# Feed-forward two slots earlier, with chunk 0's and 2's layer norm and w2's splits moved and w2's low halves on VectorE

## The chip, the cores and the metric

The kernel runs on one core of one Trainium2 chip. The metric is device time in microseconds (us) of one execution. Three runs of the kernel before were timed; their median counts. Beside them stands one profiled execution, from which all durations below come.

## The reference, cut to what matters

Inputs are 8 batches of 8 heads: 512 local queries, keys and values of width 64 per head, and 32 global ones. The result of an attention layer is mixed by a Fourier transform, normalised, and sent through a feed-forward pair of matrices.

```python
s_g = scale * q_g @ k_all^T;  out_g = sm(s_g) @ v_all          # 32 global rows see all 544 keys
s_ll = where(|i - j| <= 32, scale * q_l @ k_l^T, -1e9)          # local rows see a band
out_l = sm(concat(scale * q_l @ k_g^T, s_ll)) @ concat(v_g, v_l)
x = concat(out_g, out_l)                                        # [8, 544, 512]
u = x + real(fft(fft(x, axis=1), axis=2))
un = (u - mean(u)) / sqrt(var(u) + 1e-6)
out = u + max(un @ w_ch1, 0) @ w_ch2                            # 512 -> 2048 -> 512
```

Shapes here are those that the kernel works on (544 rows per batch).

## The kernel before, in words

**Arithmetic.** Nearly every operand of a matmul is a pair of float16 tiles, a high half (the value rounded) and a low half (what is left). A product takes three matmuls: high by high, high by low, low by high. So each operand needs a step that makes the high half (mostly ScalarE, ACT) and one that makes the low half (mostly GpSimd, POOL, for attention and weights; VectorE, DVE, for the transform and the feed-forward).

**The work.** Attention goes by 32 head pairs, each of four blocks of 128 queries; a block takes one *attention slot*. A batch has 16 slots, and six slots of pause stand after slot 15 (`A`). After the last slot of a batch (`E[b]`, attention slot 15 for batch 0, 37 for batch 1, 53 for batch 2) follows its transform: `d_load` to `d_add`, which adds the transform to x and so gives `u`. The rows of all batches are 17 *chunks* of 256 rows: chunks 2b and 2b+1 come from batch b, chunk 16 collects the rest. Each chunk has a layer norm (`l_stats`, `l_un`, `l_lo`, `l_turn`, and `l_root`, which refines the inverse root that is needed only at the end of the chunk, in `f_end`) and 16 *feed-forward slots* in 8 steps of two: `f_first` (24 matmuls, line 811), `f_hi`, `f_lo`, `f_second` (12 matmuls of 512 columns, line 830). `l_un` writes one tile of one buffer, `un`, so its second call (j = 1) waits until `l_lo` of the first has read it.

**The order.** It is written out by hand. Every step gets a time; `Plan.run` sorts by it and issues in that order, and each engine takes its own instructions strictly in that order. Times are plan slots. `add(slot, rank, ...)` puts a step at `warp(slot + rank)`, `at(time, ...)` at the time itself. `warp` leaves attention slots below `F0` as they are, stretches the next 23 over 32 plan slots, and gives two plan slots to each after those:

```python
late = F0 + 16 + PAUSE + LAG
def warp(t):
    if t < F0:
        return t
    return F0 + 32 * (t - F0) / (16 + PAUSE + LAG) if t < late else F0 + 32 + 2 * (t - late)
```

Chunk c's feed-forward begins at plan slot `F = F0 + 16 * c`; `f_first` of its step fp is at `F + 2 * fp + .30`, `f_second` at `F + 2 * fp + 3.30`. So a smaller `F0` moves all feed-forward earlier against attention: by about 2.8 plan slots of feed-forward in the stretch and four after it.

**Weights.** w1 and w2 come in as float64 bits and are turned into float32 by `w_load`, `w_abs`, `w_bits` during attention slots -11 to 30. `w_split` then scales 16 tiles of each (128x512): `w_hi` (line 252, ACT) writes the high half; for w1 POOL scales the tile and subtracts; for w2 (k = 1) ACT scales it in place (line 261) and POOL subtracts (line 262). w2's tile f is needed by `f_second` of chunk 0 in step f // 2.

**DMA.** All transfers are issued by SyncE (SP), in plan order too. `turn`, `g_turn` and `l_turn` are transposing DMAs; a DMA that waits for its source holds back those behind it on SP.

Of the kernel before, what the change touches and what calls it, by code (L numbers as in the profile page):

```python
# [13 lines left out]
AF = mybir.ActivationFunctionType  # L14
ALU = mybir.AluOpType
# [12 lines left out]
NVB = 2  # L28
NKB = 2
W0 = -8  # L30
F0 = 37
PAUSE = 6
LAG = 1
RS0 = 1.829591166069289e-20
# [41 lines left out]
class Plan:  # L76
# [3 lines left out]
    def add(self, slot, rank, fn, *a):  # L80
        self.at(self.warp(slot + rank), fn, *a)

    def at(self, time, fn, *a):
        self.q.append((time, len(self.q), fn, a))
# [6 lines left out]
class Kern:  # L91
# [163 lines left out]
    def w_split(self, k, i):  # L255
        nc = self.nc
        f, s, w = self.w_hi(k, i)
        if k == 0:
            nc.gpsimd.tensor_mul(f, f, s.to_broadcast([P, 512]))
        else:  # L260
            nc.scalar.activation(f, f, AF.Copy, scale=s)  # L261
        nc.gpsimd.tensor_sub(w[:, 1], f, w[:, 0])  # L262

    def b_load(self, b):
# [581 lines left out]
    def run(self):  # L846
        self.h = {}
# [7 lines that stand above are left out]
        plan = Plan(warp)  # L855
        add, at = plan.add, plan.at
# [3 lines left out]
        for n in range(32):  # L860
            k, t = divmod(n, 16)
            i = t if k else 4 * (t % 4) + t // 4
            s = W0 + (n if k == 0 else 16 + 3 * t // 2)
# [3 lines left out]
            if n % 4 == 3 and k == 0:  # L867
                c = n // 4
# [6 lines left out]
        add(s + 1, .62, self.w_fold)  # L875
        add(s + 2, .62, self.w_scale, 1, 0)
        for f in range(16):
            add(s + 3 + f, .75, self.w_split, 1, f)
        add(8, .09, self.load_consts)

        for b in range(B):
# [49 lines left out]
        for b in range(B):  # L931
# [32 lines left out]
            add(t + 2, .07, self.d_rest, b)  # L964
        at(F0 + 32 * 7 + 4.5, self.l_load)
        for c in range(17):
            F = F0 + 16 * c
            if c == 0:
                L, x, y, z = F - 4, (.50, .60), (.02, .06), (.30, .50)
            else:  # L970
                L, x, y, z = F - 6, (1.425, 2.425), (.335, .365), (.605, .605)
            at(L + .42, self.l_stats, c)
            for j in range(2):
                at(L + x[j], self.l_un, c, j)
                at(L + x[j] + y[1], self.l_lo, c, j)
                at(L + x[j] + z[j], self.l_turn, c, j)
            at(L + 3.43, self.l_root, c)
            for fp in range(8):
                t = F + 2 * fp
                at(t + .30, self.f_first, c, fp)  # L980
                at(t + .97, self.f_hi, c, fp)
                at(t + 1.20, self.f_lo, c, fp)
                at(t + 3.30, self.f_second, c, fp)
            for j in range(2):
                at(F + 17.82, self.f_end, c, j)
            at(F + 18.04, self.f_out, c)
# [52 lines left out]
```

## Time and profile before

| what | value |
|---|---|
| median of 3 runs | 1156.88 us |
| lowest and highest | 1155.44 and 1157.02 us |
| the profiled execution's own time | 1152.42 us |
| its span, first to last instruction | 1150.5 us |
| granted TensorE clock, mean | 0.941 |
| PE / DVE / ACT / POOL busy | 84% / 62% / 55% / 50% |
| first matmul of the feed-forward | 220.37 us |
| steps of `w_split` for w2 | 207 to 297 us |

The profile's page gives busy shares of the whole span; its rows of tenths give them by 40 slices of 28.8 us; the windows view gives busy microseconds of each engine in chosen stretches; the timeline lists instructions with their start and duration, and in brackets the idle time of the engine just before and what ended it; the chain of waits follows back from the last instruction what released what. L811 is line 811 of the kernel printed above. The profiled execution lies 4.5 us below the median of the runs.

### The profile page before, as it was taken

What the parts mean: (1) busy time and instruction counts of PE and PEld (TensorE: products, weight loads), DVE (VectorE), ACT (ScalarE), POOL (GpSimd) and SP (SyncE); (2) the same over time, 40 slices, a digit from 0 to 9 for tenths busy, and PEclk for the clock granted to TensorE, in tenths of its full rate; (3) what the DMA queues carried; (4) which work ended last, traced back from release to release, by engine and by line L of the source; (5) the groups of instructions that cost most, each with busy time, mean ns of one, the idle gap of its engine ahead of it and who ended that gap; (6) DMA issues with size and microseconds to landing.
All of it is one profiled execution on the core that took longest, in us unless ns stands there. A gap on an engine that the chain in (4) does not pass through costs nothing.

```text
span 1150.5 us, 25346 instructions
## 1 busy us (share of the span) xinstructions
PE 962.0 (84%) x9831; PEld 682.0 (59%) x9831; DVE 708.7 (62%) x1868; ACT 633.6 (55%) x1366; POOL 575.1 (50%) x728
## 2 busy tenths in 40 slices
PE   0244226588799899999999999999999999999996
PEld 0133215465576677676766676767677666666664
DVE  6997798547866865686568656866584444413211
ACT  5768558888676656665666566656564213212210
POOL 3789375778656554665465546654573312201100
PEclk9996557699899999999999999999999999999999
DMA  7578966567387465747465746573646212011100
GB/s 267 151 152 225 276 157 141 112 135 170 75 179 151 108 167 91 141 115 165 93 138 118 170 88 143 112 179 72 135 79 130 60 58 65 24 46 38 19 19 19
DMA packets 249569, 137.63 MB, mean 120 GB/s; under 512 B 200576, under 2 KB 223200, under 8 KB 249448
## 3 DMA queue, kind: packets, MB, share of 16 engines
q1 hardware_dynamic: 249448, 136.01, 51.2%
q8 instruction: 77, 1.26, 0.5%
q14 instruction: 44, 0.36, 0.1%
HBM read 65.10 MB, written 18.35 MB: 73 GB/s over the span
## 4 chain that ended last, share of the span: by engine, by line
PE 55%; DVE 24%; ACT 8%; DMA 6%; POOL 4%; issue 2%; SPq 0%; DVEq 0%; POOLq 0%; ACTq 0%
PE ps L811 22%; PE acc L830 22%; PE S L398 2%; DMA xt<-xs 2%; ACT pe L417 2%; DVE pe L408 2%; DMA qk<-in_qk 2%; PE bk L707 2%; DVE h L820 1%; PE S L468 1%; DVE ps L195 1%; DVE ps L196 1%; DVE z L328 1%; DVE wm L197 1%; DVE ps L194 1%
## 5 line engine op out<-in xcount | busy, mean ns | idle before, releaser
L811 PE MATMUL ps<-uh,wh 128*128 128x256 f16 x3264 | 383.4, 275 | 0.0
L830 PE MATMUL acc<-wh,h 128*128 128x512 f16 x1632 | 377.3, 381 | 4.1 <-DVE u L835 2.9
L811 PEld LDWEIGHTS <-wh 128*128 128x128 f16 x3264 | 319.2, 99 | 59.4 <-issue 0.7
L830 PEld LDWEIGHTS <-h 128*128 128x128 f16 x1632 | 153.5, 99 | 174.1 <-issue 9.2
L820 DVE SCALAR_TENSOR_TENSOR h<-ps,h 128x512 f16<-128x512 f32 x136 | 93.3, 686 | 188.6 <-ACT h L816 188.0
L425 POOL TENSOR_TENSOR ph<-pe,ph 128x448 f16<-128x448 f32 x128 | 137.2, 1072 | 143.0 <-ACT ph L421 88.5
L816 ACT ACTIVATE h<-ps 128x512 f16<-128x512 f32 x136 | 80.2, 589 | 223.4 <-PE ps L811 223.3
L417 ACT ACTIVATE pe<-pe,nm 128x224 f32<-128x224 f32 x256 | 102.0, 469 | 72.1 <-DVE nm L408 71.8
L408 DVE CUSTOM_DVE_ANT_0 pe<-S,msk,z 128x224 f32<-128x224 f32 x256 | 99.6, 445 | 7.5 <-PE S L398 3.6
L446 PE MATMUL bk<-vN,pl 128*128 128x65 f16 x768 | 72.9, 203 | 31.9 <-DMA pl<-ph 10.0
L398 PE MATMUL S<-kT,qT 64*128 64x192 f16 x768 | 55.7, 269 | 44.1 <-ACT pg L482 37.5
L398 PEld LDWEIGHTS <-qT 64*128 64x128 f16 x1536 | 53.7, 101 | 49.7 <-issue 38.9
L446 PEld LDWEIGHTS <-pl 128*128 128x128 f16 x768 | 62.2, 104 | 23.9 <-DMA pl<-ph 18.4
L421 ACT ACTIVATE ph<-pe 128x448 f16<-128x448 f32 x128 | 72.0, 562 | 0.0
L448 PEld LDWEIGHTS <-pl 96*128 96x128 f16 x768 | 60.1, 104 | 17.3 <-issue 10.5
L764 POOL TENSOR_SCALAR ve<-ve 128x2 f32<-128x2 f32 x17 | 5.8, 339 | 113.3 <-DVE ve L763 113.1
L376 POOL TENSOR_TENSOR kT<-qk,kT 128x512 f16<-128x512 f32 x32 | 40.7, 1272 | 36.4 <-ACT kT L371 33.0
L723 DVE SCALAR_TENSOR_TENSOR asm<-bk,dsc,asm 128x258 f32<-128x258 f32 (+1 forms) x21 | 10.1, 482 | 75.1 <-PE bk L707 60.5
L448 PE MATMUL bk<-vB,pl 96*128 96x65 f16 x576 | 55.2, 204 | 0.0
L774 ACT ACTIVATE un<-u,ve 128x512 f32<-128x512 f32 x34 | 27.6, 811 | 47.7 <-DVE unh L779 37.7
L361 ACT ACTIVATE qk<-qk,z 128x512 f32<-128x512 f32 x64 | 45.2, 708 | 10.7 <-DVE z L326 10.7
L262 POOL TENSOR_TENSOR wh<-wm,wh 128x512 f16<-128x512 f32 x32 | 38.0, 1188 | 19.7 <-ACT wm L261 18.3
(188 smaller groups left out, 1654.8 us busy)
## 6 DMA issues: line engine op xcount, KB each, us to landing
qk<-in_qk SPq DMA_DIRECT2D x32, 512.0 KB
vf<-in_v SPq DMA_DIRECT2D x32, 320.0 KB
raw<-in_moe_w_ch SPq DMA_DIRECT2D x18, 512.0 KB
xs<-x SPq DMA_DIRECT2D x32, 256.0 KB
out<-u SPq DMA_DIRECT2D x16, 512.0 KB
rw<-in_moe_w_ch SPq DMA_DIRECT2D x12, 512.0 KB
x<-xs SPq DMA_DIRECT2D x24, 256.0 KB
u<-xs SPq DMA_DIRECT2D x24, 256.0 KB
```

The lines of the kernel that those rows point to most:

```text
L361: self.nc.scalar.activation(s[nm], s[nm], AF.Copy, scale=s["z"][:, 3:4] if nm == "q" else s["z"][:, 4:5])
L398: nc.tensor.matmul(ps, qT[r, a, j], k, start=m == 0, stop=m == 2)
L408: nc.vector.tensor_tensor_reduce(self.per[(4 * p + j) % 4][:, h, 0:224], S[:, h, 224 * n:224 * n + 224], self.msk[:, j], z[:, 8:9], 3e38, ...
L417: nc.scalar.activation(pe[:, h, 0:224], pe[:, h, 0:224], AF.Exp, bias=nm[:, n, h:h + 1], scale=-1.0)
L421: self.nc.scalar.activation(ph[:, 0, :, 0:224], self.per[i % 4][:, :, 0:224], AF.Copy)
L425: self.nc.gpsimd.tensor_sub(ph[:, 1, :, 0:224], self.per[i % 4][:, :, 0:224], ph[:, 0, :, 0:224])
L446: nc.tensor.matmul(pv[:, j % 2, h], pl[:, 4 * a + 2 * h], vN[:, j, c, h, :], start=m == 0, stop=False)
L448: nc.tensor.matmul(pv[:, j % 2, h], pl[0:96, 4 * a + 2 * h + 1], vb, start=False, stop=m == 2)
L811: nc.tensor.matmul(ps[:, q], wt[:, w, c0:c0 + P], uh[:, :, 4 * a + kt, :], start=n == 0, stop=n == 11)
L816: self.nc.scalar.activation(h[:, 0], self.fps, AF.Relu)
L820: self.nc.vector.scalar_tensor_tensor(h[:, 1], self.fps, 0.0, h[:, 0], op0=ALU.max, op1=ALU.subtract)
L830: nc.tensor.matmul(self.acc_f[j], h[:, a, q, j * P:(j + 1) * P], self.w[1, f][:, w, :], start=f == 0 and a == 0 and w == 0, stop=f == 15 a ...
```

## The change

`F0` goes from 37 to 35. The low half of w2's tiles is made by one VectorE instruction, f * s - high, in place of ACT's scaling and POOL's subtraction. w2's splits are put at plan slots 33.75 + f directly, not through `warp`. Chunk 0's layer norm starts 2.82 plan slots ahead of its feed-forward (before: 4), with its two halves closer together; chunk 2's starts 4 ahead with its halves 0.1 apart (before: 6 ahead, one slot apart).

```diff
-F0 = 37
+F0 = 35
@@ w_split
         if k == 0:
             nc.gpsimd.tensor_mul(f, f, s.to_broadcast([P, 512]))
         else:
-            nc.scalar.activation(f, f, AF.Copy, scale=s)
+            nc.vector.scalar_tensor_tensor(w[:, 1], f, s, w[:, 0], op0=ALU.mult, op1=ALU.subtract)
+            return
         nc.gpsimd.tensor_sub(w[:, 1], f, w[:, 0])
@@ run
         for f in range(16):
-            add(s + 3 + f, .75, self.w_split, 1, f)
+            at(s + 3 + f + .75, self.w_split, 1, f)
@@ run
             F = F0 + 16 * c
             if c == 0:
+                L, x, y, z = F - 2.82, (.44, .50), (.02, .06), (.20, .30)
+            elif c == 2:
                 L, x, y, z = F - 4, (.50, .60), (.02, .06), (.30, .50)
             else:
                 L, x, y, z = F - 6, (1.425, 2.425), (.335, .365), (.605, .605)
```

In the last hunk `l_stats` is at L + .42, `l_un` of half j at L + x[j], `l_lo` at L + x[j] + .06 (y[1]), `l_turn` at L + x[j] + z[j], `l_root` at L + 3.43.

## Prediction

> **What bounds the kernel now.** I read the page's busy tenths first, then the windows view, then the timeline of each engine around the first feed-forward matmul, then the chain of waits up to 310 us.
>
> ```profile
> span 1150.5 us, 25346 instructions
> ...
> PE   0244226588799899999999999999999999999996
> ...
> PEclk9996557699899999999999999999999999999999
> ```
>
> The first row of tenths shows a kernel of two parts: up to about slice 10 PE is mostly idle, from there on it is full to the end. [...]
>
> ```profile
> 200.00:220.00 20.00, 6.96 (x91) 5.43 (x92) 13.12 (x42) 14.94 (x29) 13.16 (x16) 0.57 0.68 134
> 220.00:400.00 180.00, 158.93 (x1795) 113.67 (x1790) 122.69 (x338) 136.30 (x300) 125.52 (x147) 0.95 0.63 135
> 400.00:900.00 500.00, 486.76 (x5260) 345.55 (x5258) 327.00 (x879) 300.08 (x661) 278.23 (x351) 1.00 0.58 124
> 900.00:1100.00 200.00, 200.00 (x1485) 136.46 (x1485) 69.38 (x136) 43.68 (x74) 32.60 (x89) 1.00 0.15 41
> ```
>
> Columns are the stretch and its length, then busy us of PE, weight loads, DVE, ACT, POOL, then clock, DMA share, GB/s. PE idles 13.0 us in 200 to 220, 21.1 us in 220 to 400, 13.2 us in the 500 us after that, and nothing from 900 to 1100. The change leaves PE's work as it is, so the end moves by what PE's idle time changes, plus what matmuls cost at the low clock. All that can be won lies between 195 and 400 us. There the pace is set by ACT (76% busy in 220 to 400) and by engines that wait for each other.
>
> **Part 1: feed-forward two slots earlier, with chunk 0's layer norm.** These are PE's instructions around the first step:
>
> ```profile
> 219.13 0.67 PE L398 MATMUL S<-kT,qT 64*128 64x192 f16 x6 [3.25 <-ACT pg L482]
> ...
> 220.37 4.25 PE L811 MATMUL ps<-uh,wh 128*128 128x256 f16 x24
> ...
> 229.02 2.79 PE L811 MATMUL ps<-uh,wh 128*128 128x256 f16 x24
> ...
> 239.81 2.76 PE L830 MATMUL acc<-wh,h 128*128 128x512 f16 x12
> ```
>
> Scores 15 (plan slot 36.63) start at 219.13 after waiting 3.25 us for ACT; only then comes the first `f_first`, at 220.37. With F0 = 35 it is at plan slot 35.30, ahead of values 24 and scores 15, in the time when PE idles. Between scores 15 and scores 16 the new order then has two `f_first` and one `f_second` where the old one has a single `f_first`.
>
> But the layer norm that feeds it moves as well, from plan slot 33.42 to 32.60, right behind `d_add` of chunk 0 and ahead of slot 32's remaining work.
>
> ```profile
> 195.11 0.34 ACT L382 ACTIVATE kg<-gT,z 128x64 f16<-128x64 f16 x1
> ...
> 203.09 0.81 ACT L774 ACTIVATE un<-u,ve 128x512 f32<-128x512 f32 x1 [2.76 <-POOL ve L767]
> ...
> 205.32 0.82 ACT L774 ACTIVATE un<-u,ve 128x512 f32<-128x512 f32 x1 [0.76 <-DVE unh L779]
> ```
>
> ```profile
> 196.96 0.74 POOL L732 TENSOR_TENSOR u<-u,asm 128x255 f32<-128x255 f32 x1
> ...
> 202.84 0.21 POOL L767 TENSOR_SCALAR ve<-ve 128x2 f32<-128x2 f32 x1
> ```
>
> ```profile
> 198.60 0.69 DVE L760 BATCH_NORM_STATS2 bst<-u 128x6 f32<-128x512 f32 x1
> ...
> 207.22 0.68 DVE L779 TENSOR_TENSOR unh<-un,unh 128x512 f16<-128x512 f32 x1
> ```
>
> Before, ACT waits 2.76 + 0.76 = 3.5 us in the layer norm. In the new order its `l_un` stands right behind line 382, which ends at 195.45. POOL finishes chunk 0's u at 197.70; from DVE's first statistics (198.60) to POOL's last step (203.05) took 4.45 us, of which one half's 0.69 + 0.18 can go before 197.70, so the bias is there between 199.9 (nothing blocked) and 201.3. I take 200.0: ACT waits 4.5 us. Its second `l_un` waits for `l_lo`, which on DVE now stands behind w_scale, norm 10 and the four masked rows of slot 32; I estimate 2.3 us from their order. Together 6.8 us, 3.3 more than before. Queued behind it on ACT are prep_hi and sums of slot 32, `d_as`, exps 13, p_hi 25 and g_hi 6; DVE's `d_df` of the next block, PE's `d_second`, and scores 14 wait for those. POOL's three small steps move ahead of prep_lo, p_lo 25 and g_lo 6. On SP the two `l_turn` move ahead of turn 24, whose values are a slot and a half away on PE, so I put that at nothing, and at up to 1 us if that cover is gone. `l_root` goes to plan slot 35.61 and is needed only in `f_end`, over 16 slots later: nothing.
>
> ACT saves the three in-place scalings that stand ahead of scores 15 and gets one `f_hi`. The prices:
>
> ```profile
> L261 ACT ACTIVATE wm<-wm,wsc x16: 721/722/724, 207.4 to 295.4; 128x512 f32<-128x512 f32 x16
> ...
> L636 DVE SCALAR_TENSOR_TENSOR eh<-s,dsc,eh x8: 732/744/1525, 173.2 to 957.8; 128x512 f16<-128x512 f32 x8
> ...
> 362.84 0.58 ACT L816 ACTIVATE h<-ps 128x512 f16<-128x512 f32 x1
> ```
>
> So scores 15 move by 3.3 - 3 x 0.72 + 0.58 (an `f_hi`) = +1.7, to 220.8, and end at 222.1. Then PE does 2 x 2.79 + 2.76 = 8.3 us of feed-forward and about 3.3 us of values, global values and scores (the 8.65 us from 220.37 to 229.02 hold 4.25 of `f_first`, 2.1 us of waiting and some 2.3 of these; slot 26 and 27 with scores 16 make a little more in the new order): scores 16 end at 233.7, 4.7 us later than the 229.02 of before, but 8.3 us of feed-forward are ahead. **Term 1: -3.6 us**, from 0 (the layer norm costs another 3.6) to -6 (ACT's wait no longer than before and the POOL wait gone).
>
> **Part 2: w2's splits.** Sixteen ACT instructions of 0.722 us and sixteen POOL subtractions go; sixteen DVE instructions come. Line 636 has the same operation, size and types as the new one: 0.744 us. What of it lies on the path is to be read from the chain of waits:
>
> ```profile
> 273.60 1.16 POOL wh L262
> ...
> 294.67 0.73 ACT wh L252
> 295.43 0.72 ACT wm L261
> ```
>
> Three splits are in part 1; thirteen remain, 13 x 0.722 = 9.4 us off ACT and 13 x 1.16 = 15.1 us off POOL. Of that 1.16 + 0.73 + 0.72 = 2.6 us stand in the chain in the stretch where PE is worst fed (the last two because a split stands at plan slot 53; now all are done by 48.75, ahead of batch 1's transform). Between 220 and 245 more ACT pieces of splits stand in it, but other waits are next there. **Term 2: -3 us**, from 0 to -9.4 (all of ACT's time on the path).
>
> DVE gets 13 x 0.744 = 9.7 us in a stretch in which it idles 57 us of 180 (122.69 busy), so the work itself is covered; without that cover it would cost the 9.7. Each new instruction waits for ACT's high half, and masked rows, f_lo and g_max are queued behind it; but it stands 0.75 of a slot in, when DVE mostly waits for ACT anyway. The row of line 636 goes up to 1.525 us. [...] **Term 3: +0.3 us**, from 0 to +10 (13 x 0.78, the most by that row, all on the path).
>
> **Part 3: chunk 2.** With F0 = 35 `d_add` of batch 1 falls at 62.23 instead of 61.45, chunk 2's statistics stay at 63.42, its first matmul goes from 69.30 to 67.30: 5.07 slots from `d_add`, not 7.86.
>
> ```profile
> 331.34 0.84 POOL L731 TENSOR_TENSOR u<-u,asm 128x257 f32<-128x257 f32 x1 [1.90 <-DVE asm L724]
> ```
>
> From `d_add` (331.34) to the first `f_hi` of chunk 2, less a `f_first` of 2.8, are 28.7 us, 3.65 us per slot; 5.07 slots are 18.5 us. The chain needs 1.19 slots to the statistics (4.3 us), chunk 0's 9.3 us from 198.60 to the end of the second low half (207.90), and the transposing DMA, which I put at 3 to 4 us: 16.6 to 17.6. It just fits. ACT waits inside it as in chunk 0 (3.5 us), where ACT has a quarter of its time free. **Term 4: +1 us**, from 0 to +6. Even chunks from 4 on keep their layer norm, but `d_add` comes 1.28 slots ahead of the statistics, not 5.28; 4.7 us cover POOL's two adds of 0.84: nothing, at most 2 either way.
>
> **Part 4: the clock.** The first `f_first` took 4.25 us at the low clock, later ones 2.79. One such step stays. In the new order PE idles some 3 us between it and scores 15, so the second may be slow as well: **term 5: +0.7 us**, from 0 to +1.5. [...]
>
> **The sum:** -3.6 - 3 + 0.3 + 1 + 0.7 = -4.6 us. The profiled execution would go from a span of 1150.5 to 1145.9; its own time is 1152.42, 4.5 us below the median of the runs, and I carry the difference over: 1156.88 - 4.6 = 1152.3. About 0.2%, 2.3 us, can be told from no change.
>
> **The rivals.**
> (a) The layer norm gives all of term 1 back. For it: ACT is the pace maker at 200 to 245, and 6.8 us of waiting is my own estimate from the order. Against it: three scalings leave ACT at the same place. Then -3 + 2 = -1: 1156, no change to be told. Chance 0.14.
> (b) Slower: chunk 2's first matmul comes before its transposed rows. For it: the margin is 1 to 2 us. Against it: no slot of 3.65 us has to be lost for the chain to fit. It decides when the chain of part 3 passes 18.5 us, against 16.6 to 17.6 needed; then PE, which takes its queue in order, stands still for the excess. If the four DVE instructions in it take twice their 0.7 us, as line 636's slowest did, and ACT and SP reach it a slot late each (2 x 3.65), the chain is 17.6 + 2.8 + 7.3 = 27.7 us: 9.2 us of PE idle, so -4.6 - 1 + 9.2 = +3.6: 1160.5. Chance 0.12.
> (c) The new DVE instructions are blocked by POOL each time and hold the masked rows: 13 x 0.78 = 10.1 us, half of it on ACT's path, +5: 1157.3. Chance 0.05.
> (d) The splits are what feeds PE badly: all 9.4 us of ACT's time come off the path, -4.6 - 6.4 = -11: 1145.9. For it: ACT's share of the stretch; against: only 2.6 us of splits in the chain of waits after 245. Chance 0.14.
> (e) The forecast as worked out, within about 3 us: 0.55.
>
> **How the numbers follow.** Faster by over 0.2% holds (d) and most of the forecast, 0.66; within 0.2% (a), part of (c) and the forecast's upper edge, 0.19; slower (b) and part of (c), 0.15. The range takes in (a), (c) and (d) with an upper and lower edge of some 1.5 to 3 us beside them, and stops just short of (b): 1144.5 to 1160.
>
> **What would show it.** Right: the first L811 at about 211 to 213, slow; scores 15 at 220 to 222 with ACT idle some 4 us and 2 us ahead of its two L774; the new instructions at 0.75 to 1.5 us with no long wait of PE behind them; no PE wait at the first `f_first` of chunk 2; PE idle in 200 to 400 down by 4 to 6 us and unchanged after that. Wrong: scores 15 beyond 224, or a wait for the transposed rows at chunk 2, or PE idle that reappears after 400, where even chunks now follow their transform closely.

## The result, and the profile after

The change made the kernel slower: 1166.08 us median (1164.46 to 1169.2, 4 runs) against 1156.95 of the kernel before in the same comparison, a ratio of 1.0088, 95% interval 1.0065 to 1.0111. Forecast were 1152.3 and a range up to 1160.0.

The profiled execution of the changed kernel took 1169.2 us, 3.1 above its median, and that of before 4.5 below, so the two profiles differ by 16.8 us where the medians differ by 9.1. Differences between the two traces are read here for places and kinds; sizes come from the runs. The line numbers shown from 262 on are higher by one in the changed kernel.

The page (PEclk is the granted clock by slice, in tenths) and the windows view of the changed kernel, in the columns used for before:

```profile
span 1167.4 us, 25360 instructions
...
PE   0234326598689999989998999899989999999996
...
PEclk9999998699899999999999999999999999999998
```

```profile
200.00:220.00 20.00, 9.66 (x129) 8.02 (x128) 16.31 (x45) 10.39 (x21) 9.31 (x12) 0.67 0.53 86
220.00:400.00 180.00, 156.04 (x1762) 111.47 (x1762) 121.04 (x344) 124.34 (x279) 102.02 (x123) 0.93 0.62 138
400.00:900.00 500.00, 480.82 (x5089) 338.70 (x5087) 311.28 (x872) 302.17 (x667) 277.89 (x353) 0.98 0.56 121
900.00:1100.00 200.00, 199.00 (x1580) 136.38 (x1578) 74.41 (x161) 46.12 (x85) 38.64 (x86) 1.00 0.20 51
```

PE idles 10.3 us in 200 to 220 (13.0 before), 24.0 in 220 to 400 (21.1), and 19.2 in 400 to 900 (13.2). In the third row the granted clock is 0.98, not 1.00. The forecast looked for all of the effect ahead of 400 us; that part came out about even (34.3 us of idle time against 34.1), and the loss sits in the stretch that was taken to be full.

**Ahead of 310 us** the forecast steps happened, with two stalls that the forecast did not have. The first feed-forward step starts 8.8 us earlier, but scores 15 come 7.5 us later (219.13 before):

```profile
211.56 3.04 PE L812 MATMUL ps<-uh,wh 128*128 128x256 f16 x24
...
226.62 0.67 PE L399 MATMUL S<-kT,qT 64*128 64x192 f16 x6 [2.98 <-ACT pg L483]
```

ACT's waits in chunk 0's layer norm, from its timeline, are 4.5 and 1.3 us, close to the 4.5 and 2.3 worked out:

```profile
201.04 0.81 ACT L775 ACTIVATE un<-u,ve 128x512 f32<-128x512 f32 x1 [4.50 <-POOL ve L768]
...
203.80 0.81 ACT L775 ACTIVATE un<-u,ve 128x512 f32<-128x512 f32 x1 [1.29 <-DVE unh L780]
```

The extra stall stands in `scales` of group 4, eight tiny VectorE steps. First DVE's timeline of before, then that of the changed kernel, then POOL's of the changed kernel:

```profile
206.47 0.16 DVE L328 SCALAR_TENSOR_TENSOR z<-z 128x2 f32<-128x2 f32 x1
206.55 0.22 DVE L329 TENSOR_SCALAR z<-z,ge 128x2 f32<-128x2 f32 x1
206.81 0.17 DVE L330 TENSOR_SCALAR z<-z 128x4 f32<-128x4 f32 x1
```

```profile
209.73 0.98 DVE L329 SCALAR_TENSOR_TENSOR z<-z 128x2 f32<-128x2 f32 x1
210.64 2.72 DVE L330 TENSOR_SCALAR z<-z,ge 128x2 f32<-128x2 f32 x1
213.39 1.15 DVE L331 TENSOR_SCALAR z<-z 128x4 f32<-128x4 f32 x1
```

```profile
210.66 1.27 POOL L489 TENSOR_TENSOR pgr<-pg,pgr 64x576 f16<-64x576 f32 x1
211.89 0.73 POOL L732 TENSOR_TENSOR u<-u,asm 128x257 f32<-128x257 f32 x1
212.58 0.72 POOL L733 TENSOR_TENSOR u<-u,asm 128x255 f32<-128x255 f32 x1
213.27 1.24 POOL L341 TENSOR_TENSOR vf<-vf,z 128x640 f32<-128x640 f32 x1
```

Four of the eight steps, the three shown and the one behind them, last until a GpSimd instruction ends (at 210.69, 213.30, 214.51 and 215.50); the other four take 0.16 to 0.22 us. ACT's delay had held back POOL's work (p_lo 25, g_lo 6, `d_add`), which then came in one burst on top of `scales`: from 209.13 to 215.66 they take 6.5 us, where before they took 1.4 (205.88 to 207.31) and POOL stood idle beside them.

The second stall is PE's longest wait behind 200 us, in front of the scores at 304.42:

```profile
304.42 0.67 PE L399 MATMUL S<-kT,qT 64*128 64x192 f16 x6 [10.07 <-ACT pg L483]
```

The longest wait of before there was 6.04 us, at 290.64. In the changed kernel VectorE waits 4.74 us ahead of it for the transfer that `d_load` of batch 1 starts; before it waited 0.62.

**From 400 us on** the view of PE's waits says what is new. Its columns: who waited for whom, us in total, times, longest. First before, then the change, for 400 to 880 us:

```profile
PE bk L446 <- DVE xg L513: 5.4, 4, 1.4
PE bk L677 <- DVE x L459: 5.1, 3, 2.0
PE S L398 <- ACT pg L482: 1.9, 2, 1.6
```

```profile
PE S L399 <- ACT pg L483: 17.6, 5, 3.5
PE bk L447 <- DVE xg L514: 1.6, 4, 0.4
```

Several waits of 1 to 2 us became one of 3.52 us in each batch. One of the five, rows of three timelines of the changed kernel:

```profile
515.97 0.21 POOL L765 TENSOR_SCALAR ve<-ve 128x2 f32<-128x2 f32 x1 [10.24 <-DVE ve L764]
...
516.73 2.35 POOL L594 TENSOR_TENSOR s<-x 128x1020 f32<-128x1020 f32 x1
```

```profile
519.11 2.04 DVE L598 TENSOR_TENSOR x<-x 128x1020 f32<-128x1020 f32 x1 [3.23 <-POOL s L594]
```

```profile
525.43 0.42 PE L399 MATMUL S<-kT,qT 64*128 64x192 f16 x6 [3.52 <-ACT pg L483]
...
526.17 4.41 PE L831 MATMUL acc<-wh,h 128*128 128x512 f16 x12
```

Line 765 is the first of GpSimd's three small steps in the layer norm of chunk 5; it waits 10.24 us for VectorE's statistics. Behind it in GpSimd's queue stands `d_odd` (594), the transform step of batch 3, which is thereby late; VectorE's `d_even` (598) overwrites what `d_odd` reads and waits 3.23 us for it, and then takes 2.04 us beside GpSimd's next instructions; behind `d_even` on VectorE stands the maximum of the global scores, behind that ACT's exponential, behind that PE. With F0 = 37 these statistics (plan slot 111.42) stood behind `d_odd` and `d_even` (107.7 and 107.9). With F0 = 35 they are at 109.42, while the transform, two slots later against the feed-forward, has `d_tail` at 108.6, `d_odd` at 109.71 and `d_even` at 109.88: the statistics have come to stand right ahead of them. By the plan this holds for the odd chunks 3 to 13 (behind chunk 15 no transform follows); the five waits belong to chunks 3 to 11, and behind 900 us no scores are left to wait.

Against the kernel before, the loss is not spread evenly, because that kernel had waits of its own. From the first `f_hi` of an even chunk to that of the next even one, the two profiles have 115.2 us before and 115.4 after (chunks 4 to 6), 114.6 and 115.5 (6 to 8), 113.5 and 116.3 (8 to 10), 104.2 and 113.0 (10 to 12). In the last of these PE did not wait at all before, and part of the difference there seems to be attention work that the smaller `F0` leaves for later: with the statistics 0.6 later the same stretch takes 107.9 us with a wait of only 0.55.

### The profile page after: what moved, and what is told of

Read it like the earlier page. It is cut to its first block, busy times and chain, and to the rows that moved or that the text cites. A ratio compares the mean times of both kernels' runs of the same rounds, so it can differ in the third digit from the quotient of the medians.

```text
span 1167.4 us, 25360 instructions
## 1 busy us (share of the span) xinstructions
PE 970.7 (83%) x9831; PEld 685.8 (59%) x9831; DVE 700.7 (60%) x1884; ACT 622.4 (53%) x1350; POOL 555.1 (48%) x712
## 4 chain that ended last, share of the span: by engine, by line
PE 58%; DVE 22%; ACT 7%; POOL 6%; issue 3%; DMA 3%; SPq 0%; POOLq 0%; DVEq 0%; ACTq 0%
PE acc L831 25%; PE ps L812 23%; PE S L399 2%; DVE pe L409 2%; ACT pe L418 1%; PE bk L708 1%; POOL s L594 1%; DVE h L821 1%; DVE ps L195 1%; DVE x L598 1%; DVE ps L194 1%; DVE ps L196 1%; PE bk L447 1%; DVE wm L197 1%; PE bk L678 1%
## 5 line engine op out<-in xcount | busy, mean ns | idle before, releaser
L831 PE MATMUL acc<-wh,h 128*128 128x512 f16 x1632 | 386.3, 388 | 1.0 <-DVE h L821 1.0
L780 DVE TENSOR_TENSOR unh<-un,unh 128x512 f16<-128x512 f32 x34 | 32.6, 958 | 33.2 <-ACT unh L776 33.2
L352 POOL TENSOR_TENSOR vN<-vf,vN 128x640 f16<-128x640 f32 x32 | 48.8, 1524 | 3.5 <-ACT vN L348 3.5
L377 POOL TENSOR_TENSOR qT<-qk,qT 128x512 f16<-128x512 f32 x32 | 37.8, 1182 | 17.0 <-ACT qT L372 17.0
```

The source lines that it names most:

```text
L377: self.nc.gpsimd.tensor_sub(lo, s.pop(nm), hi)
L831: nc.tensor.matmul(self.acc_f[j], h[:, a, q, j * P:(j + 1) * P], self.w[1, f][:, w, :], start=f == 0 and a == 0 and w == 0, stop=f == 15 a ...
```

## The experiments

Theory T, in its short form: the loss comes from the place of layer norms, the odd chunks' above all, between steps of the transform, and not from the splits or from the early feed-forward itself. Rivals: R1, the new VectorE instructions; R2, F0 = 35 as such.

**The splits alone, and the change without them.** To the kernel before only these two edits:

```diff
-            nc.scalar.activation(f, f, AF.Copy, scale=s)
+            nc.vector.scalar_tensor_tensor(w[:, 1], f, s, w[:, 0], op0=ALU.mult, op1=ALU.subtract)
+            return
-            add(s + 3 + f, .75, self.w_split, 1, f)
+            at(s + 3 + f + .75, self.w_split, 1, f)
```

> The kernel before (F0 = 37, its layer norms) with only the two edits to w2's splits: low halves by one VectorE instruction, splits at plan slots 33.75 + f. Theory T (the loss comes from two collisions around layer norms: chunk 0's, which lets GpSimd run into the small VectorE steps of scales 4, and the odd chunks', whose statistics now stand between the transform's tail and d_odd): the splits alone save 1 to 5 us, 1152 to 1156 us. Rival R1 (the new VectorE instructions, blocked by GpSimd, are the cost): most of the +9 us is here, 1162 to 1167 us.

Measured: 1151.75 us, ratio 0.9965 (0.9948 to 0.9982), 4.5 us below the kernel before and just below T's range. The ratio is to the kernel before, as timed beside each run; its median went from 1155.1 to 1158.0 us between these comparisons, so differences of 1 or 2 us between runs of different comparisons can't be told from none. The reverse, the changed kernel with the first of these edits undone:

> The changed kernel with w2's low halves made by ScalarE and GpSimd as before; F0, layer norms and the splits' slots stay changed. Theory T: not faster than the changed kernel, 1166 to 1172 us, with the waits of 3.5 us for ACT in each batch still there. Rival R1: the +9 us go away, 1156 to 1160 us.

Measured: 1173.23 us, ratio 1.0149 (1.0118 to 1.018), 7 us above the changed kernel and just above T's range, with the five waits of 3.5 us unchanged. R1 falls: both edits to the splits gain 4.5 us in the kernel before, and the low halves on VectorE alone some 7 us in the changed one. The row of the new instructions in the changed kernel (shortest, median and longest in ns) shows that only some of them are held up:

```profile
L261 DVE SCALAR_TENSOR_TENSOR wh<-wm,wsc,wh x16: 732/752/1756, 216.2 to 281.6; 128x512 f16<-128x512 f32 x16
```

**Chunk 0's layer norm at its old place.** In the changed kernel:

```diff
-                L, x, y, z = F - 2.82, (.44, .50), (.02, .06), (.20, .30)
+                L, x, y, z = F - 2, (.50, .60), (.02, .06), (.30, .50)
```

> The changed kernel with chunk 0's layer norm back at the plan slots it had before (statistics at 33.42, halves at 33.5 and 33.6, transposes at 33.8 and 34.1). Theory T: the small steps of scales 4 run in some 1.5 us again instead of 6, scores 15 come 4 to 6 us earlier, 1159 to 1163 us. Rival R2 (feed-forward that starts two slots earlier is too early whatever the layer norm does, as the first matmul only waits): 1165 to 1168 us.

Measured: 1162.26 us, ratio 1.0054 (1.0034 to 1.0074). The eight steps of `scales` take 1.4 us again (206.93 to 208.36), and scores 15 come at 222.78, 3.8 us earlier. The first feed-forward matmul now waits 8.35 us for its transposed rows, so it starts later (214.31 against 211.56), and still the whole is 3.8 us faster: what counts at this place is attention's pace, not the first matmul. The two intervals overlap a little (that of the changed kernel begins at 1.0065), but the slowest of these runs, 1163.34 us, lies below the fastest of the changed kernel, 1164.46.

**The odd chunks' statistics 0.6 plan slots later.** In the changed kernel:

```diff
-            at(L + .42, self.l_stats, c)
+            at(L + (1.02 if c > 2 and c % 2 else .42), self.l_stats, c)
```

> The changed kernel with the statistics of odd chunks from 3 on 0.6 plan slots later, so behind d_odd and d_even of the next batch's transform instead of ahead of them. Theory T: the five waits of scores for ACT of 3.52 us shrink to under 1.5 us each, 1155 to 1161 us. Rival R2: the waits come from the transform itself, which now falls against the chunk's end; they stay, 1164 to 1168 us.

Measured: 1145.05 us, ratio 0.9913 (0.9888 to 0.9939): 21 us below the changed kernel, more than T expected. The waits did not stay, so the rival R2 of this run falls. The waits view of this run, 400 to 880 us:

```profile
PE S L399 <- ACT pg L483: 5.9, 5, 1.4
```

The waits fell by 11.7 us in five batches; most of the rest is the clock. The windows view (PE busy, granted clock, DMA share, GB/s) of the 5.6 us behind one wait, in the changed kernel, then behind the same wait in this run:

```profile
525.40:531.00 5.60, 5.57 (x42) 0.70 0.76 109
```

```profile
516.80:522.40 5.60, 5.50 (x56) 1.00 0.57 112
```

Behind this wait of 3.52 us PE went on at 0.70 of its clock, behind the one of 1.30 us at 1.00. So this wait cost its length and, by an estimate from the window, about half as much again: 0.3 x 5.6 = 1.7 us. In the 5.6 us behind the other four waits the granted clock was 0.70, 0.70, 0.52 and 0.53. The matmuls bear it out: `f_second` right behind the five waits took 3.80, 4.41, 4.45, 4.79 and 4.77 us instead of 2.76, together 8.4 us more, and 11.7 + 8.4 = 20.1 of the 21 us. With 2.2 us of wait saved that is 3.9 us per batch; the period from chunk 4 to chunk 6 (first `f_hi` to first `f_hi`) went from 115.4 to 111.6 us.

**The mirror: the same collision at F0 = 37.** In the kernel before, this one edit:

```diff
-            at(L + .42, self.l_stats, c)
+            at(L + (-3.58 if c > 2 and c % 2 else .42), self.l_stats, c)
```

> The kernel before with one edit: the odd chunks' statistics from 3 on four plan slots earlier, which puts them between the transform's tail and d_odd, where the change has them. Theory T (that place is the cost, not F0 = 35): scores wait 3 us or more for ScalarE in each batch, the granted clock drops below 1.00 in 400 to 880 us, and the time goes up by 4 to 12 us, 1160 to 1169 us. Rival R2 (the early feed-forward is the cost): 1155 to 1159 us.

Measured: 1169.94 us, ratio 1.0103 (1.0052 to 1.0154). The waits view, 400 to 880 us:

```profile
PE S L398 <- ACT pg L482: 16.3, 4, 4.6
PE bk L446 <- DVE xg L513: 5.4, 4, 1.4
```

The chain is the same down to the wait of `d_even` for `d_odd`, from VectorE's timeline:

```profile
508.50 2.04 DVE L597 TENSOR_TENSOR x<-x 128x1020 f32<-128x1020 f32 x1 [3.23 <-POOL s L593]
```

The slow-down, 12.0 us, appears without any change of F0 or of the splits, with the same kind of wait (four of them, up to 4.6 us) and a clock of 0.98. It is just above the range of T. R2, F0 = 35 as such, falls.

**Which queue carries it.** In the changed kernel the statistics go behind `d_odd` on GpSimd but stay ahead of `d_even` on VectorE:

```diff
-            at(L + .42, self.l_stats, c)
+            at(L + (.80 if c > 2 and c % 2 else .42), self.l_stats, c)
```

> The changed kernel with the odd chunks' statistics 0.38 plan slots later: behind d_odd (GpSimd) but still ahead of d_even (VectorE). If GpSimd's queue is the mechanism (its three small layer norm steps wait for VectorE's statistics and hold d_odd, which then runs into VectorE's own steps), the wait of scores for ScalarE falls to 1 to 2 us per batch and the time to 1143 to 1149 us, as with the place behind both. If the 1.9 us of statistics ahead of d_even on VectorE are the mechanism, the wait stays at 3 us or more and the time at 1160 to 1166 us.

Measured: 1142.97 us, ratio 0.9893 (0.9865 to 0.9922). The waits view, 400 to 880 us:

```profile
PE S L399 <- ACT pg L483: 3.3, 4, 0.8
```

VectorE's order around `d_even` is unchanged, but now `d_even` follows the statistics at once, from VectorE's timeline:

```profile
511.70 1.24 DVE L598 TENSOR_TENSOR x<-x 128x1020 f32<-128x1020 f32 x1
```

The waits came out shorter than the 1 to 2 us expected, at most 0.8, and the time just below the range. So the mechanism is GpSimd's queue: `d_odd` behind three small steps that wait for VectorE. The statistics' own time on VectorE ahead of `d_even` does not bring the waits back. Whether this place is better than the one behind both is not shown: 1142.97 and 1145.05 us come from different comparisons, and the intervals of their ratios overlap.

**Adding up.** The changed kernel with chunk 0's layer norm at its old place and the statistics 0.6 later:

> The changed kernel with both moves: chunk 0's layer norm at its old plan slots and the odd chunks' statistics 0.6 slots later. Theory T (two separate collisions, one ahead of the saturated part, one in every batch of it): the two gains add up, 20 us and 4 us below the changed kernel, 1139 to 1143 us. Rival R3 (both moves free the same slack): not below 1144 us.

Measured: 1141.63 us, ratio 0.9871 (0.9832 to 0.9911), 3.4 us below the statistics alone. The intervals overlap, but no run of one reaches those of the other (up to 1143.20, from 1144.13 on). R3's bound of 1144 is not reached, which speaks for two separate places. A place for chunk 0's layer norm between the two, with the statistics 0.6 later:

```diff
-                L, x, y, z = F - 2.82, (.44, .50), (.02, .06), (.20, .30)
+                L, x, y, z = F - 2.3, (.50, .60), (.02, .06), (.20, .40)
```

> The changed kernel with the odd chunks' statistics 0.6 slots later and chunk 0's layer norm between its two places (statistics at 33.12, behind exps 13 and ahead of the next transform block). Theory T: the small steps of scales 4 stay at 1.5 us, as ScalarE gets slot 32's work done first, and the first feed-forward matmul waits less than the 8.35 us that it waits for the transposed rows with the late place: 1137 to 1142 us. Rival: any wait of ScalarE for the layer norm ahead of scales 4 brings the collision back, 1144 to 1147 us.

Measured: 1141.63 us, ratio 0.9871 (0.9832 to 0.9911), the same as with the late place. `scales` took 3.6 us there (207.22 to 210.78), between 1.4 and 6.5, and PE waited only 0.90 us for the rows. The time lies in T's range, but T's reason, `scales` at 1.5 us, did not come: a part of one loss stands against the other.

Batch 1's `d_load` 0.9 attention slots earlier, with the statistics 0.6 later:

```diff
-            add(R + 8, .09, self.d_load, b)
+            add(R + (7.1 if b == 1 else 8), .09, self.d_load, b)
```

> The changed kernel with the odd chunks' statistics 0.6 slots later, and batch 1's d_load 0.9 attention slots earlier. The longest PE wait left in it is 10.3 us at 300 us, behind a VectorE wait of 4.7 us for xt. If the transfer is what is late there, the wait falls to 5 or 6 us and the time to 1138 to 1142 us. If VectorE and GpSimd blocking each other in the transform's tail set it, the wait stays above 9 us and the time at 1144 to 1147 us.

Measured: 1142.65 us, ratio 0.9879 (0.984 to 0.9918). PE's wait near 300 us went from 10.3 to 6.6 us, not quite to the 5 or 6 expected, and VectorE no longer waits for the transfer: it was late. What is left is VectorE and GpSimd in the transform's tail. From VectorE's timeline of this run:

```profile
284.45 7.89 DVE L644 TENSOR_TENSOR st<-xt 32x255 f32<-32x255 f32 x1
```

This step took 0.41 us in the kernel before. Here it lasts until 292.34, beside six GpSimd instructions one right behind the other (284.08 to 292.06). All three moves together:

> The changed kernel with the odd chunks' statistics 0.6 slots later, chunk 0's layer norm at its old plan slots and batch 1's d_load 0.9 attention slots earlier. The last two gave 3.4 and 2.4 us each on top of the first. If they are separate places, 1138 to 1141 us, below both kernels and the lowest here; if the earlier transfer only fills the time that the later layer norm leaves, 1141 to 1143 us.

Measured: 1138.03 us, ratio 0.9859 (0.9823 to 0.9894). The time is in the range for separate places, but the kernel before ran faster too in this comparison; by the ratios the third move adds 0.1 to 0.2% (0.9871 and 0.9879 with two), which is within the intervals. So whether all three add up stays open. And with the statistics at .80:

> The changed kernel with the odd chunks' statistics 0.38 slots later, chunk 0's layer norm at its old plan slots and batch 1's d_load 0.9 attention slots earlier. Against the same with 0.6 slots (1138.0 us) theory T expects the 2 us that separated the two places before: 1134 to 1138 us.

Measured: 1137.10 us, ratio 0.9832 (0.9812 to 0.9853): in the range, but 0.9 us below the other in place of 2, from another comparison, so the two places of the statistics still can't be told apart.

**Chunk 2.** In the changed kernel PE's longest wait between 320 and 400 us belongs to chunk 2's layer norm, though not at the place that the prediction watched. Timelines of DVE and PE:

```profile
349.53 0.69 DVE L780 TENSOR_TENSOR unh<-un,unh 128x512 f16<-128x512 f32 x1 [2.42 <-ACT unh L776]
```

```profile
351.07 0.33 PE L708 MATMUL bk<-c2r,z 128*18 128x129 f16 x3 [3.62 <-DVE asm L725]
```

Chunk 2's low half waits on VectorE for ACT, `d_df` of batch 1 stands behind it, and PE's `d_second` waits for `d_df`. To the kernel last named:

```diff
-                L, x, y, z = F - 4, (.50, .60), (.02, .06), (.30, .50)
+                L, x, y, z = F - 4, (.65, .75), (.02, .06), (.30, .50)
```

> As the kernel run beside it (e12), with the two halves of chunk 2's layer norm 0.15 plan slots later, so that its low halves stand behind d_df of batch 1's second block on VectorE instead of ahead of it. Theory T (the only PE wait above 3 us that is left behind 320 us, 3.62 us of d_second for d_df, is VectorE held by chunk 2's low half, which waits for ScalarE): the wait goes and the low clock behind it, 3.5 to 5.5 us below e12. Rival: d_df would be late anyway, or chunk 2's first matmul is then late for its transposed rows: within 1.5 us of e12.

Measured: 1135.32 us (1133.17 to 1137.94), ratio 0.9827 (0.9801 to 0.9853), against 1137.10 (1134.76 to 1138.33) beside it. The wait of 3.62 us went, but the next `d_second` then waited 3.74 us for ACT's `d_as`, queued behind the layer norm there. The difference of 1.8 us lies within the scatter of the two; whether this edit gains stays open. It is, with the kernel beside it, the fastest here, some 1.7% below the kernel before.

## Why the prediction was wrong, point by point

- **What bounds the kernel**: PE is nearly full from 400 us on, as it says. But "All that can be won lies between 195 and 400 us" is wrong both ways. A stretch that is full can be made less full, and this change moved steps in every batch of it; and with the statistics out of the way PE's idle time from 400 to 880 us is 7.9 or 5.2 us (statistics 0.6 or 0.38 later) against 13.2 before. The granted clock did not follow PE's idle time alone: in the row of before the first three slices have 9 with PE at 0, 2 and 4 tenths; from 28.76 to 86.30 us it was 1.00 with PE busy for 19.80 of the 57.54 us, from 115.0 to 172.6 us 0.50 with 15.13 of 57.60; and in the changed kernel's profile the first six slices have 9.
- **Part 1, order and waits**: right in its places (first `f_first` 211.6 against 211 to 213; ACT's waits 5.8 in sum against 6.8), wrong in its sum. Scores 15 were put at 220.8 and came at 226.6, 1.1 of which the run had lost by slot 30 already. What the working left out is that POOL's delayed burst would fall on `scales`: 5.1 us. This and what hangs on it cost 3.4 to 3.8 us of the total, about as much as term 1 (-3.6) was to gain. That is rival (a) by its effect; its reason, ACT's waiting, was there at the size foreseen and not larger. The forecast also has no term for the longer wait at 304 us, behind the late transfer; with the transfer moved the time was 2.4 us lower (1142.65 against 1145.05, with intervals that overlap).
- **Part 2, term 2 and 3**: sign right, size a little low. -3 + 0.3 was forecast for the thirteen splits, -4.5 (both edits alone) and -7 us (the low halves, inside the change) measured for the sixteen. The new instructions took 0.752 us in the median and 1.756 at most, so rival (c) was not what happened. The +0.3 of term 3 was the author's estimate, and no run shows it by itself.
- **Part 3, the failed step**: "Even chunks from 4 on keep their layer norm, but `d_add` comes 1.28 slots ahead of the statistics, not 5.28 ... nothing, at most 2 either way." It asked only whether a layer norm's inputs are ready. It did not ask what stands behind the layer norm on each queue, and it passed over the odd chunks, whose inputs are early, altogether. There the statistics' new neighbours were `d_odd` and `d_even` of the next batch. What was put at "nothing, at most 2" measured 21 to 23 us, more than the whole miss of 13.8 (1166.1 against 1152.3): without it the same change is 11 to 12 us faster than before. The sum's other gaps are small beside it.
- **Term 4, chunk 2** (+1, range to 6): the first matmul of chunk 2 did not wait, so rival (b) did not happen, but 3.62 us of PE waiting arose at `d_second` of batch 1; the net of it was not settled. The 3 to 4 us for the transposing DMA were the author's estimate: before, SP's record of the second transpose of chunk 0 ends at 211.83, 3.9 us behind the second low half (207.90); with chunk 0's layer norm at its old place the matmul that waits for the transposed rows starts at 214.31, 5.4 us behind that half (208.95).
- **Part 4, term 5, the clock**: about right where it was looked for. The first two `f_first` took 3.04 and 5.09 us (granted clock 0.91 and 0.54) against 4.25 and 2.79 before (0.65 and 1.00), together 1.1 us more where 0.7 was forecast, though the slow one was the second and not the first. That some 3 us of idle time ahead of it could make the second slow was the author's estimate: PE waited 1.72, 4.38 and 2.98 us between the two, and no run shows which of these brought the clock down. The clock mattered far more in the full stretch, where the forecast had no term for it: 8.4 us in the five `f_second` behind the waits, 1.7 each on average.
- The gain without the collision, 11 to 12 us, is larger than the forecast's 4.6. The kernel before had waits of its own in the full stretch (12.4 us in the three rows above), which the new alignment, once the statistics are out of the way, replaces by 4.9 to 7.6; that is 5 to 8 us. How the rest divides among the parts was not measured, so a sum near -4.6 would have been in part luck.

## What to carry to other kernels

When one constant shifts one schedule against another, list for every step that keeps its place in one of them what its new neighbours on each in-order queue are, over a whole period and not only where the change starts. Small steps that wait for another engine (here three GpSimd instructions of 0.2 us) are the ones to look at: their price is what stands behind them. In a stretch that looks full, 2.2 us more of one wait cost 3.9 here, since the granted clock behind it was 0.70 in place of 1.00.

## What the runs showed of the hardware that was not expected

A VectorE step of 0.22 us (line 330, two elements per partition) took 2.72 us while GpSimd ran three instructions one after another (210.66 to 213.30), and one of 0.41 us (line 644, with `d_load` earlier) took 7.89 us beside six of them. The first ended at 213.36, 0.06 us behind the third GpSimd instruction, and not behind the first or second (211.93 and 212.62); the other ended at 292.34, behind the sixth (292.06). Why these steps were held so long and others beside GpSimd were not, no run here shows.

The clock behind a PE wait, by the windows of 5.6 us behind it: 0.70, 0.70, 0.70, 0.52 and 0.53 behind the five waits of 3.52 us; 1.00 behind 1.30; and in the kernel before 0.70 behind 2.03 us (at 526.9) but 1.00 behind 1.94 (at 756.3). No run here shows a length of wait from which on it goes down.
